# A fused attention block: set-up rebuilt, two GpSimd chains and a new plan

## The chip, the cores and the metric

The kernel runs on one NeuronCore of a Trainium2 chip. The metric is the time of one execution on the device in microseconds. Before the change it is 406.25 us, the median of three runs (406.25 to 406.31). The profile shows one execution, from its first to its last instruction.

## The reference

x is 1 x 2048 x 448 in bf16, with 16 heads of 28 columns each:

```python
qkv = (x @ wqkv).reshape(B, S, 3, H, Dh).transpose(2, 0, 3, 1, 4)
q, k, v = qkv[0], qkv[1], qkv[2]
scores = einsum("bhqd,bhkd->bhqk", q, k) * Dh ** -0.5
p = softmax(scores, axis=-1)
o = einsum("bhqk,bhkd->bhqd", p, v)
return o.transpose(0, 2, 1, 3).reshape(B, S, D) @ wo
```

## The kernel before

**Tiling.** The heads stand in 4 groups of 4, each head padded to 32 rows. The 2048 queries are 4 blocks of 512. A window is one group and one query block, so there are 16 windows; each has 16 key tiles of 128, and for each key tile 4 heads. A score tile is 128 keys by 512 queries of one head: 1024 tiles in all. TensorE (PE) computes a tile with one matmul over 64 rows (L935): 32 rows are the head's key and query, the other 32 hold the absolute query and a negative bound on the key, so that the score arrives with an upper bound already subtracted and no row maximum is needed. After the exponential a matmul with the values (L1203) adds into the bank PO. A column of ones in the values gives the denominators.

**Three ways to the exponential.** Most tiles go in pairs through a PA bank pair, and ScalarE (ACT) takes the exponential of 128x1024 (L1364, into PTA). A part goes through a PD bank: VectorE (DVE) makes two passes of a polynomial (DU L1139, DV L1142), GpSimd (POOL) multiplies (DG L1145), and DVE finishes into PTD (L1158). For the third kind DVE only copies the score into SG (L1071) and GpSimd does the rest as a chain of six: GU (L1078), GE (L1081), GV (L1084), GU (L1086), SG (L1088), PTD (L1101). `start_g` makes that chain. There is one set of GU, GV, GE, so one chain at a time (`GMAX = 1`, `NG = 3` copies of SG), and none starts before 40 tiles have been issued (`GBEG`).

**Set-up.** The blocks of x are called b = 0 to 3. Blocks 0 to 2 are loaded as XS and transposed by PE (L462) into XT; block 3 comes transposed by DMA. The loads are issued on SP's queue (x0, WQ, x1, x2, WV, block 3), WK alone on ACT's queue. GpSimd pads WK into WKP (L425), ACT pads WQ into WQP (L426). DVE fills constants before, among them the unit rows of XT and the ones in VA (L359, L360). For key block 0, PE makes K (L578) and Q (L714), DVE reduces the largest |k| to KPART (L587), ACT copies the two Q halves (L730, L732) and the two masked key copies (L599, L596); DVE and GpSimd form |q| times the bound into QB (L738, L749, L746). The first two windows run first over key block 0 alone, four heads for each key tile; the bound over all keys (KMAX L630, NK L635) follows while they run, and DMAs copy keys and bound rows to the other partitions (L641, L652). `task_factor` (FW, negm, RR L997) corrects the first two partial sums to the common bound.

**Order.** Nothing is scheduled by hand. While the program is built, an event loop plays the whole kernel through: each `Op` has an engine, a length, the latency of its result, and what it depends on; per-window numbers in `PLAN` set priorities, leads and thresholds. At each instant `try_pe`, `try_act` and `try_static` choose an instruction for a free engine, and the order so found is what each engine executes. On the chip, semaphores keep the dependencies, and each engine works through its list in order. At a POOL operation the loop adds `TDEP` where it follows the one it depends on. A DVE operation of kind `sb` (SBUF to SBUF, such as QP) and a GpSimd operation are kept apart by `port` and `lock`.

**End.** The last window normalizes on DVE by transposes (L947 to L1509), and the remaining output matmuls use banks that have come free; ACT and DVE copy, SP and ACT issue the stores.

```python
op = Op("ACT", 0.0633 + 0.4267 * len(ns), fn, kind="E", lat=ELAT)
cp = add(Op("DVE", CPY, lambda: nc.vector.tensor_copy(out=X[:], in_=PX[slot.idx][:]), deps=[sop], ...))
if o.kind == "g" and (pool_last[0] in o.deps or o.dur == PTS and o.acq is None):
    o.dur += TDEP
```

Of the kernel before, what the change touches and what calls it, by code (L numbers as in the profile page):

```python
# [21 lines left out]
P = 128  # L22
# [10 lines left out]
KEPS = 1e-6  # L33
# [19 lines left out]
    "LEADC": [30, 0, 39, 26, 16, 30, 14, 14, 37, -2, 23, 43, 34, 20, -3, 13],  # L53
    "PVMORE": [3, 9, 6, 1, 2, 5, 3, 4, 4, 3, 2, 6, 2, 2, 0, 8],
    "QFROM": [8, 0, 13, -18, 2, -7, -14, -3, -29, 0, 15, -30, 2, 27, 2, 20],
    "QBY": [64, 33, 84, 35, 80, 63, 48, 35, 70, 68, 37, 26, 24, 83, 73, 82],
    "QLEAD": [-88, 27, 38, -61, -3, -56, 48, 32, 6, -83, 0, 17, 28, -85, -90, 11],
    "KFROM": [34, 11, 29, -12, -10, -8, 19, 19, 18, 30, 41, -14, 27, 26, 8, 2],
    "KBY": [23, 12, 48, -4, 29, 50, 40, 54, 30, -2, 2, 49, 14, 48, 9, 40],
    "KLEAD": [34, 27, -74, -63, -7, -50, 32, 24, 1, -25, -43, -62, 18, -27, -8, 47],  # L60
    "VFROM": [-2, 8, 7, 30, -2, 49, 8, 15, 40, -1, -5, 24, 46, -9, 35, 43],
    "VBY": [41, 25, 52, 0, 56, 14, 11, 57, 57, 37, 59, 4, 57, -8, 17, 49],
    "VLEAD": [48, 73, 0, -21, 9, -23, 6, 54, 46, 20, 21, -27, -34, 9, -21, -1],
    "NORM": [20, 10, -10, 38, 6, 40, 20, 10, -14, -4, 9, -10, -18, 20, 32, -1],
    "TAIL": [8, 8, 40, 1],
    "PART": [-34, -19, 34, 37, -30, 40, 3, 30],
    "OUT": [0, 10, 28, 39, 20, -22, 7, -6, 5, -8, -2, 39, -30, -10, 13, 39],
    "SLK": [0.2, 0.22, 0.21, 0.19, 0.12, 0.21, 0.2, 0.12, 0.24, 0.11, 0.08, 0.22, 0.17, 0.19, 0.27, 0.12],
# [6 lines left out]
TDEP = 0.12  # L75
WDR = 0.117
VREL = 0.3
# [10 lines left out]
EVU = 0.598  # L88
DISS = 0.6
# [6 lines left out]
class Op:  # L96
    __slots__ = ("eng", "dur", "lat", "deps", "fn", "prio", "elig", "acq", "rel", "end", "start", "kind", "after")

    def __init__(self, eng, dur, fn, deps=(), prio=0.0, elig=None, acq=None, rel=None, lat=SEM, kind=None, after=None):
        self.eng, self.dur, self.fn, self.deps, self.prio = eng, dur, fn, list(deps), prio  # L100
        self.elig, self.acq, self.rel, self.lat, self.kind, self.after = elig, acq, rel, lat, kind, after
        self.end = None
        self.start = None
# [14 lines left out]
def kernel(  # L118
# [29 lines left out]
    NG = 3  # L148
    GMAX = 1
# [6 lines left out]
    GBEG = 40  # L156
# [35 lines left out]
    FE2 = 80  # L192
# [3 lines left out]
    TE = 0  # L196
    CPE = 1
    REDP = 0
    TW = 0
    XLAT = (4.6, 7.3, 8.9, 9.6)  # L200
    WQLAT = 5.9
    XSP = 1
    KP0 = -4377
    KP1 = -4375
    KP2 = -4485
    BP2 = 34
    PBND = ((3,), (2, 3))
    VE = 16
    UV = 4
    BW = (-1, 4, 1)  # L210
    THF = (0, 1, 0, 0)
    EVP = (-1200, -4365, -700, 0)
    KEVP = (0, 200, 200, 200)
    WQE = 'ACT'
    QORD = 0
    KCH = ((1, 2), (2, 4))
    RCH = ((1, 4), (0, 1))
    XT3 = 14.0
    XBAR = True
    KENG = ('ACT', 'DVE', 'DVE', 'DVE')  # L220
    HENG = ('ACT', 'DVE', 'DVE', 'DVE')
# [24 lines left out]
    RK0 = sb([P, 1], F32, "RK0")  # L246
# [3 lines left out]
    VA = [sb([P, NKT, HG, HP], BF16, f"VA{g}") for g in range(G)]  # L250
# [35 lines left out]
    maskm = sb([P, QW], BF16, "maskm")  # L286
# [3 lines left out]
    bndcol = [sb([P, 1], F32, f"bndcol{pr}") for pr in range(2)]  # L290
    mcol = sb([P, 1], F32, "mcol")
    bdiff = sb([P, 1], F32, "bdiff")
    negm = sb([P, NF, HP], BF16, "negm")
# [5 lines left out]
    nc.scalar.dma_start(out=WK[:, :, 0:GW], in_=wq3[:, :, D:D + GW])  # L299
    for b in range(NQC):  # L300
        if b < NQC - 1:
            nc.sync.dma_start(out=XS[b][:], in_=x_perm[:, b * TPC:(b + 1) * TPC, :])
# [23 lines left out]
    for i in range(HG):  # L326
        nc.gpsimd.affine_select(out=onescol[:], in_=onescol[:], compare_op=ALU.not_equal, fill=1.0,
                                base=-(HP * i + Dh), pattern=[[0, 1]], channel_multiplier=1)
    for g in range(G):
# [4 lines left out]
    UB = 96  # L334
# [13 lines left out]
    nc.gpsimd.tensor_scalar(out=mcol[:], in0=onescol[:], scalar1=MARG, scalar2=-MARG, op0=ALU.mult, op1=ALU.add)  # L348
    nc.gpsimd.tensor_tensor(out=bdiff[:], in0=onescol[:], in1=mcol[:], op=ALU.subtract)
    for pr in range(2):  # L350
# [338 lines left out]
    def task_Q(g, c):  # L689
# [30 lines left out]
        if w == 0:  # L720
            k0mm.extend(ops)
# [826 lines left out]
```

## Time and profile before

| what | value |
|---|---|
| time, median of three | 406.25 us |
| span of the profiled execution | 404.5 us |
| first exponential starts | 11.87 us |
| last exponential ends | 396.9 us |
| exponentials on ACT | 419 (418 of 128x1024, one of 128x512) |
| tiles through DVE and GpSimd / through GpSimd alone | 162 / 25 |
| busy: PE, DVE, ACT, POOL | 353.5, 387.5, 393.5, 345.0 us |
| granted TensorE clock | 0.999 |

The profiled execution's own time is not recorded apart from its span; the three timed runs agree within 0.06 us, so the span is set against their median, and 1.75 us lie around it. In a group's row stand line, engine, operation, the written tile, an arrow and the tiles read, shapes and count; then busy microseconds, the mean of one in ns, the idle time just before, and what ended it. A timeline row has start and length in us, then how many instructions follow each other, and in brackets the idle time before and its releaser. Lengths of neighbours overlap by some tens of ns.

### The profile page before, as it was taken

How to read it: one execution, taken by the hardware profiler on the slowest of the kernel's cores; microseconds unless marked ns; L12 is line 12 of the kernel's file. 1: busy time of each engine (PE TensorE's matmuls, PEld its weight loads, DVE VectorE, ACT ScalarE, POOL GpSimd, SP SyncE). 2: the span in 40 equal slices, each digit the busy share in tenths (PEclk: the TensorE clock that was granted, in tenths of full speed). 3: DMA queues.
4: the chain of work that ended last, by engine and by line, in shares of the span. 5: the costliest groups of instructions: out<-in, count | busy, mean ns of one | idle time of the engine just before them, and what ended most of it. 6: DMA issues, size and time to landing. Idle time of an engine off the chain costs nothing.

```text
span 404.5 us, 7615 instructions
## 1 busy us (share of the span) xinstructions
PE 353.5 (87%) x2596; PEld 115.6 (29%) x2607; DVE 387.5 (96%) x700; ACT 393.5 (97%) x432; POOL 345.0 (85%) x370
## 2 busy tenths in 40 slices
PE   7999979998898888899888987888898898989896
PEld 4342332322232232322322232222223322222232
DVE  6989999999999999999999999999999999999995
ACT  5999999999999999999999999999999999999994
POOL 3429999879899889899999899988899997989990
PEclk9999999999999999999999999999999999999999
DMA  9351120212301020110411000010220002001012
GB/s 212 51 85 42 47 55 26 36 44 40 68 2 47 0 53 7 18 41 2 101 39 33 24 20 10 1 48 1 71 56 16 32 2 56 11 26 51 5 69 91
DMA packets 36446, 16.58 MB, mean 41 GB/s; under 512 B 28784, under 2 KB 33136, under 8 KB 36408
## 3 DMA queue, kind: packets, MB, share of 16 engines
q1 hardware_dynamic: 35800, 15.89, 16.8%
q8 instruction: 20, 0.33, 0.3%
q10 hardware_dynamic: 608, 0.22, 0.2%
q14 instruction: 18, 0.15, 0.1%
HBM read 7.44 MB, written 1.97 MB: 23 GB/s over the span
## 4 chain that ended last, share of the span: by engine, by line
ACT 42%; DVE 23%; PE 15%; POOL 10%; issue 7%; DMA 1%; SPq 0%; DVEq 0%; POOLq 0%
ACT PTA L1364 42%; PE PA L935 6%; DVE PTD L1158 6%; DVE DU L1139 5%; DVE DV L1142 5%; POOL DG L1145 5%; PE PO L1203 4%; PE PD L935 2%; POOL GU L1086 1%; POOL SG L1088 1%; PE PO L714 1%; DMA QB<-QP 1%; DVE SG L1071 1%; POOL OSB L1011 1%; POOL PTD L1101 1%
## 5 line engine op out<-in xcount | busy, mean ns | idle before, releaser
L1364 ACT ACTIVATE PTA<-PA 128x1024 bf16<-128x1024 f32 x419 | 384.5, 1165 | 0.8 <-PE PA L935 0.6
L935 PE MATMUL PA<-QB,KB 64*128 64x512 bf16 x837 | 168.5, 381 | 39.5 <-ACT PTA L1364 36.0
L1145 POOL TENSOR_TENSOR DG<-DV,DU 128x512 f16<-128x512 f16 x162 | 185.1, 1154 | 16.8 <-DVE DV L1142 11.9
L935 PEld LDWEIGHTS <-KB 64*128 64x128 bf16 x1024 | 61.5, 93 | 181.7 <-issue 173.6
L1158 DVE SCALAR_TENSOR_TENSOR PTD<-PD,DG 128x512 uint16<-128x512 f32 x162 | 109.0, 679 | 3.1 <-POOL DG L1145 2.0
L1142 DVE SCALAR_TENSOR_TENSOR DV<-PD,DU 128x512 f16<-128x512 uint16 x162 | 107.9, 680 | 0.8
L1139 DVE TENSOR_SCALAR DU<-PD 128x512 f16<-128x512 uint16 x162 | 106.8, 677 | 1.9 <-PE PD L935 1.7
L1203 PE MATMUL PO<-PTA,VA 128*32 128x512 bf16 x837 | 83.1, 385 | 0.1
L935 PE MATMUL PD<-QB,KB 64*128 64x512 bf16 x187 | 68.6, 377 | 3.5 <-DVE PTD L1158 2.0
L1203 PE MATMUL PO<-PTD,VA 128*32 128x512 bf16 x187 | 53.6, 386 | 0.0
L1203 PEld LDWEIGHTS <-VA 128*32 128x32 bf16 x1024 | 18.8, 94 | 46.5 <-issue 44.9
L1086 POOL TENSOR_TENSOR GU<-GV,GU 128x512 f16<-128x512 f16 x25 | 28.9, 1154 | 2.2 <-DVE QP L762 1.5
L1088 POOL TENSOR_TENSOR SG<-SG,GU 128x512 f32<-128x512 f32 x25 | 28.9, 1155 | 1.9 <-DVE QP L762 0.8
L1084 POOL TENSOR_TENSOR GV<-GE,GU 128x512 f16<-128x512 f32 x25 | 28.9, 1156 | 1.7 <-DVE QP L762 0.8
L1038 POOL TENSOR_TENSOR OT<-OSB,RRB 128x512 bf16<-128x512 f32 x15 | 19.0, 1270 | 1.5 <-DVE PTD L1158 1.5
L1078 POOL TENSOR_SCALAR GU<-SG 128x512 f16<-128x512 uint16 x25 | 15.4, 617 | 5.1 <-DVE SG L1071 3.4
L1071 DVE COPY SG<-PD 128x512 f32<-128x512 f32 x25 | 17.0, 681 | 0.5 <-PE PD L935 0.3
L714 PE MATMUL PO<-XT,WQP 112*128 112x512 bf16 (+1 forms) x52 | 16.9, 385 | 0.3 <-DVE OSB L1023 0.3
L1081 POOL TENSOR_SCALAR GE<-SG 128x512 f32<-128x512 uint16 x25 | 15.4, 617 | 2.0
L578 PE MATMUL PO<-XT,WKP 112*128 112x512 bf16 (+1 forms) x52 | 16.9, 385 | 0.1
L794 PEld LDWEIGHTS <-XT 112*128 112x128 bf16 x256 | 13.6, 98 | 10.7 <-issue 10.4
L1101 POOL TENSOR_SCALAR PTD<-SG 128x512 uint16<-128x512 f32 x25 | 15.5, 618 | 0.9
(120 smaller groups left out, 197.4 us busy)
## 6 DMA issues: line engine op xcount, KB each, us to landing
RRB<-SCR SPq DMA_DIRECT2D x15, 256.0 KB
QB<-QP SPq DMA_DIRECT2D x56, 32.0 KB
KB<-NK SPq DMA_DIRECT2D x12, 128.0 KB
XS<-in_x_dram SPq DMA_DIRECT2D x3, 448.0 KB
QB<-QB SPq DMA_DIRECT2D x28, 32.0 KB
out_dram<-XS SPq DMA_DIRECT2D x2, 448.0 KB
KB<-KB SPq DMA_DIRECT2D x6, 128.0 KB
RRB<-SCRF SPq DMA_DIRECT2D x2, 256.0 KB
```

The lines of the kernel that those rows point to most:

```text
L714: ops = chain_mm(CC, lambda cc: nc.tensor.matmul(out=ap(), lhsT=WQP[g][0:rows_of(g, c, cc), cc, :], rhs=XT[c][cc // 2][0:rows_of(g, c, cc) ...
L935: nc.tensor.matmul(out=ap, lhsT=KB[g % 2][i // 2][a:a + 64, j * P:(j + 1) * P], rhs=QB[w % NQB][i // 2][a:a + 64, :], start=True, stop=Tru ...
L1071: cp = add(Op("DVE", CPY, lambda: nc.vector.tensor_copy(out=X[:], in_=PX[slot.idx][:]), deps=[sop], prio=n - PLAN["LEADC"][now()], lat=0.165))
L1084: g3 = add(Op("POOL", PTT, lambda: nc.gpsimd.tensor_tensor(out=GV[:], in0=GE[:], in1=GU[:], op=ALU.mult), deps=[g2], prio=prio + 2, kind=" ...
L1086: g4 = add(Op("POOL", PTT, lambda: nc.gpsimd.tensor_tensor(out=GU[:], in0=GV[:], in1=GU[:], op=ALU.mult), deps=[g3], prio=prio + 3, kind=" ...
L1088: g5 = add(Op("POOL", PST, lambda: nc.gpsimd.tensor_tensor(out=X[:], in0=X[:], in1=GU[:], op=ALU.add), deps=[g4], prio=prio + 4, kind="g", ...
L1139: p1 = add(Op("DVE", P1, lambda: nc.vector.tensor_scalar(out=DU[b][:], in0=lo, scalar1=SIG / 65536, scalar2=SIG * (SS - 0.5), op0=ALU.mult ...
L1142: p2 = add(Op("DVE", P1, lambda: nc.vector.scalar_tensor_tensor(out=DV[b][:], in0=lo, scalar=65536 * (SS - 0.5 + CE / C3), in1=DU[b][:], o ...
L1145: gq = add(Op("POOL", PTT, lambda: nc.gpsimd.tensor_tensor(out=DG[b][:], in0=DV[b][:], in1=DU[b][:], op=ALU.mult), deps=[p2], prio=n, kind ...
L1158: f = add(Op("DVE", P1, lambda: nc.vector.scalar_tensor_tensor(out=PTD[st["s"].idx][:].bitcast(U16), in0=PX[slot.idx][:], scalar=EBITS + C ...
L1203: nc.tensor.matmul(out=PO[HP * st:HP * (st + 1), :], lhsT=VA[g][:, j, st, :], rhs=r["p"][i][1](), start=first, stop=last, tile_position=(0 ...
L1364: nc.scalar.activation(out=PTA[pslot.idx][:, 0:len(ns) * QW], in_=PA[s.idx][:, 0:len(ns) * QW], func=ACT.Exp, bias=ACT_BIAS, scale=ACT_SCALE)
```

## The change

- **Loads.** WK is issued on SP's queue, after x0 and ahead of WQ.
- **Padding and constants.** GpSimd pads WK in two halves and WQ whole. The unit rows of XT and the ones in VA move from DVE to GpSimd, written as 32-bit words; VA has two buffers in place of four, so values of group g wait for the weighted sums of group g-2.
- **Block 0 of x** is transposed and copied in four column pieces, three copied by DVE and one by ACT, and each key and query matmul waits for its piece alone.
- **Bounds.** The first block's |q| is no longer multiplied by the key bound; the bound is a column (`bndcol`, two sets) which `masked_evac` puts into the key copy, for block 0 by DVE in pieces of 128 and 384 columns, for block 1 by DVE after the overall maximum. Copying key block 1 by DMA falls away; the repeats of NK for it too.
- **Query blocks.** For window 0 ACT evacuates one half and forms |q| of one head; DVE does the others. The second query block is evacuated twice from PSUM instead of copied in SBUF.
- **First windows.** The first two windows run heads 0 and 1 over four key tiles, then heads 2 and 3.
- **GpSimd chains.** Two sets of GU, GV, GE (`NCH = 2`), `GMAX = 2`, `NG = 4`, chains from 58 tiles on.
- **Planner.** A GpSimd operation carries the class of its first scalar (`cls`); a change of class costs `PSW`. Operations of a chain wait for their predecessor's latency. Lists are kept sorted and searched in that order. `PLAN` is new.

```diff
-    nc.scalar.dma_start(out=WK[:, :, 0:GW], in_=wq3[:, :, D:D + GW])
         if b == 0:
+            nc.sync.dma_start(out=WK[:, :, 0:GW], in_=wq3[:, :, D:D + GW])
             nc.sync.dma_start(out=WQ[:, :, 0:GW], in_=wq3[:, :, 0:GW])
...
-    for b in range(NQC - 1):
-        nc.vector.memset(XT[b][1][UB:CK + 2, 1, :], 1.0)
-    nc.vector.memset(VA[0][:].rearrange("p j h e -> p (j h) e")[:, :, Dh:HP], 1.0)
+    nc.gpsimd.memset(XT[0][1][UB:CK + 2, 1, :].bitcast(F32), ONES2)
...
+    for cc in range(CC):
+        tv = xbank[cc].bitcast(BF16)
...
+        tro = add(Op("PE", 0.22, tr0, deps=[xs_in], prio=-5000 + cc, lat=0.1, kind="T"))
...
+        xt_done[0].append(add(Op(XE[cc], 0.41 if XE[cc] == "DVE" else 0.58, ev0, deps=[tro], prio=-5000 + cc, lat=0.08)))
...
+    kpads = [add(Op("POOL", 0.33, pad_half(ch), deps=[wkin], prio=-5001 + 0.1 * ch, lat=0.1)) for ch in range(2)]
+    w_ready[("q", 0)] = add(Op("POOL", 0.57, pad_w(WQ, WQP, 0), deps=[wqin], prio=-4999, lat=0.1))
...
+    def masked_evac(k, sc, ap, dep, kmax, pb, p0, p1):
+        bcs = []
+        for i in range(HG):
+            st = SI[i]
+            eng = nc.gpsimd if k else nc.vector
+            bcs.append(add(Op("POOL" if k else "DVE", 0.21, lambda st=st, eng=eng: eng.tensor_scalar(
+                out=bndcol[k][st % 2][HP * (st ^ 1):HP * ((st ^ 1) + 1), :], in0=kmax[HP * st:HP * (st + 1), :],
+                scalar1=mcol[HP * st:HP * (st + 1), 0:1], scalar2=0.0, op0=ALU.mult, op1=ALU.add), deps=dep, ...
+        def ev(pr, a, b, prio, elig=None):
+            return add(Op("DVE", 0.065 + EVC * (b - a), lambda: nc.vector.tensor_scalar(
+                out=KB[0][pr][:, sc * QW + a:sc * QW + b], in0=ap()[:, a:b], scalar1=selcol[pr][:, 0:1], scalar2=bndcol[k][pr][:, 0:1], op0=ALU.mult, op1=ALU.add),
+                deps=bcs[2 * pr:2 * pr + 2], prio=prio, elig=elig))
+        if k:
+            return [ev(pr, 0, QW, p1 if pr else p0) for pr in range(2)]
+        return [ev(0, 0, P, p0), ev(0, P, QW, -4387.5, ...), ev(1, 0, P, p1), ev(1, P, QW, -4355)]
...
+            ab = add(Op("ACT", 0.62, lambda: nc.scalar.activation(
+                out=QB[0][0][HP:2 * HP, :], in_=ap[0:HP, :], func=ACT.Abs, scale=YSC), deps=[ops[-1]], prio=-4389, lat=0.17))
...
-    KCH = ((1, 2), (2, 4))
-    RCH = ((1, 4), (0, 1))
+    KCH = ((2, 4),)
+    RCH = ((2, 4), (0, 1))
...
-    NG = 3
-    GMAX = 1
+    NG = 4
+    NCH = 2
+    GMAX = 2
...
+        ch = g_seq[0] % NCH
         g_seq[0] += 1
+        U, V, E = GU[ch], GV[ch], GE[ch]
...
-                    if o.kind == "g" and (pool_last[0] in o.deps or o.dur == PTS and o.acq is None):
-                        o.dur += TDEP
+                    if o.cls:
+                        if o.cls != pool_cls[0]:
+                            o.dur += PSW
```

More of the change, by code (lines that the diff above doesn't have):

```diff
@@ L533 @@
     rep0s = []
[L534 to L535 removed]
+    k0ev0 = []
+    neg_op = []
     SI = (0, 2, 1, 3)
```

471 lines of the change are left out of this document (230 added, 241 removed), and 6 rows, old and new, of the table PLAN.

## The prediction

> **What bounds the kernel now.** I read the page first (shares, groups), then ScalarE's (ACT's) timeline, then the busy time by stretch, and last the timeline of the set-up.
>
> ```profile
> span 404.5 us, 7615 instructions
> PE 353.5 (87%) x2596; PEld 115.6 (29%) x2607; DVE 387.5 (96%) x700; ACT 393.5 (97%) x432; POOL 345.0 (85%) x370
> L1364 ACT ACTIVATE PTA<-PA 128x1024 bf16<-128x1024 f32 x419 | 384.5, 1165 | 0.8 <-PE PA L935 0.6
> L1145 POOL TENSOR_TENSOR DG<-DV,DU 128x512 f16<-128x512 f16 x162 | 185.1, 1154 | 16.8 <-DVE DV L1142 11.9
> L1142 DVE SCALAR_TENSOR_TENSOR DV<-PD,DU 128x512 f16<-128x512 uint16 x162 | 107.9, 680 | 0.8
> L1084 POOL TENSOR_TENSOR GV<-GE,GU 128x512 f16<-128x512 f32 x25 | 28.9, 1156 | 1.7 <-DVE QP L762 0.8
> L1078 POOL TENSOR_SCALAR GU<-SG 128x512 f16<-128x512 uint16 x25 | 15.4, 617 | 5.1 <-DVE SG L1071 3.4
> L1071 DVE COPY SG<-PD 128x512 f32<-128x512 f32 x25 | 17.0, 681 | 0.5 <-PE PD L935 0.3
> ```
>
> ```profile
> 11.87 24.26 ACT L1364 ACTIVATE PTA<-PA 128x1024 bf16<-128x1024 f32 x26 [0.62 <-PE PA L935]
> 35.98 0.65 ACT L997 ACTIVATE RR<-PO 128x512 f32<-128x512 f32 x1
> 36.45 360.44 ACT L1364 ACTIVATE PTA<-PA 128x1024 bf16<-128x1024 f32 x393
> 398.22 0.53 ACT L898 CAST XS<-PA 128x448 bf16<-128x448 f32 x1 [1.33 <-PE PA L897]
> ```
>
> ```profile
> 37.00:387.00 350.00, 307.32 (x2244) 97.41 (x2254) 344.66 (x596) 349.88 (x383) 320.42 (x318) 1.00 0.13 32
> ```
>
> The 1024 score tiles have three ways to their exponential: in pairs on ACT (419 instructions), through DVE and GpSimd together (162 tiles), through one DVE copy and then GpSimd alone (25). From 11.87 us to 36.45 + 360.44 = 396.89 us ACT does nothing but exponentials, one per 360.44 / 393 = 0.917 us, with a single other instruction (L997) between. So the span is three terms: 11.87 us until the first exponential, 385.0 us of them, and 7.6 us of tail. The last fence (columns: PE, weight loads, DVE, ACT, POOL busy) shows what stands close behind: in 350 us DVE is idle for 5.3 us, GpSimd for 29.6 us. The granted clock is 1.00.
>
> **The change, term by term.**
>
> *1. Until the first exponential.* These rows carry the set-up:
>
> ```profile
> 0.73 0.42 ACTq L299 DMA_DIRECT2D WK<-in_wqkv_dram  x1
> 0.74 0.40 SPq L302 DMA_DIRECT2D XS<-in_x_dram  x1
> 4.56 1.57 DVE L359 MEMSET XT<- 18x512 bf16 x3
> 4.64 0.88 PE L462 MATMUL PD<-ident,XS 128*112 128x128 bf16 x12 [0.17 <-DMA XS<-in_x_dram]
> 5.09 0.56 POOL L425 COPY WKP<-WK 112x448 bf16<-112x448 bf16 x1 [0.36 <-DVE XT L359]
> 5.98 0.58 ACT L475 COPY XT<-PD 112x512 bf16<-112x512 bf16 x1
> 6.23 0.27 DVE L360 MEMSET VA<- 128x256 bf16 x1
> 6.42 0.63 DVE L473 COPY XT<-PD 112x1024 bf16<-112x1024 bf16 x1
> 6.96 0.41 DVE L473 COPY XT<-PA 112x512 bf16<-112x512 bf16 x1
> 7.10 0.59 PE L578 MATMUL PD<-XT,WKP 112*128 112x512 bf16 x2 [1.36 <-DVE XT L473]
> 7.53 1.02 PE L714 MATMUL PD<-XT,WQP 112*128 112x512 bf16 x4
> 8.39 0.59 PE L578 MATMUL PD<-XT,WKP 112*128 112x512 bf16 x2
> 8.59 0.69 ACT L730 ACTIVATE QB<-PD,offscol 128x512 bf16<-128x512 f32 x1 [2.03 <-PE PD L714]
> 8.82 0.61 PE L462 MATMUL PA<-ident,XS 128*112 128x128 bf16 x8
> 9.02 0.69 DVE L587 TENSOR_REDUCE KPART<-PD 128x1 f32<-128x512 f32 x1 [1.65 <-PE PD L578]
> 9.18 0.68 ACT L732 ACTIVATE QB<-PD,offscol 128x512 bf16<-128x512 f32 x1
> 9.83 0.15 DVE L592 TENSOR_SCALAR KPART<-KPART 128x1 f32<-128x1 f32 x1
> 10.01 1.79 DVE L749 TENSOR_SCALAR QB<-QP,KPART 32x512 bf16<-32x512 bf16 x3
> 10.48 0.77 ACT L596 ACTIVATE KB<-PD,bndcol,selcol 128x512 bf16<-128x512 f32 x1
> 11.46 0.37 PE L935 MATMUL PA<-QB,KB 64*128 64x512 bf16 x1 [0.37 <-DVE QB L749]
> ```
>
> The transposes of x start at 4.64, when it has landed; WK's 98 KB run beside it, from ACT's queue. Behind x they leave it alone: nothing gained at the least, at the most WK's share at the rate of that moment,
>
> ```profile
> 3.00:4.00 1.00, 1.00 (x4) 0.36 (x3) 0.93 (x7) 1.00 (x1) 0.72 (x6) 1.00 1.06 327
> ```
>
> 98 KB / 327 GB/s = 0.3 us. I take 0.2: start at 4.44. The price is WK itself, which now lands after x; its padding (0.56 us, halved into two) could end 0.5 us later than 5.65 and still precede the use below.
>
> Now DVE's four memsets (4.56 to 6.50) stand before its first copy of transposed x. They go to GpSimd (the first block's ahead of time, the rest behind the weight padding), so DVE copies as the transposes come. Sixteen of them take 0.88 + 0.39 less overlap, 1.1 us, four to a column piece: the pieces are there at about 4.9, 5.1, 5.3 and 5.6; DVE copies three (0.41 each), ACT one (0.58), and the last ends at 6.07 against 7.37 now. The key matmuls follow (their order puts all four ahead of the query's) and end at 6.1 + 0.4 = 6.55 against 8.98. The absolute maximum (0.69) ends at 7.3. Two small bound columns (0.15 each as in L592) and a 128-column piece of the key copy, a quarter of a 0.7 us copy plus its fixed part, say 0.25, end near 8.0 on DVE. That was 0.78 + 0.77 on ACT.
>
> On the other branch the four query matmuls (1.02) end at 7.4; ACT evacuates the first half (0.69, to 8.15) and takes |q| for one head, 0.6 behind it as L732 stands 0.59 behind L730: 8.75. This replaces QP, the floor and the multiplications by the key bound, 1.79 for three. The first score pair runs at 8.8, and the exponential follows 11.87 - 11.46 = 0.41 later: **9.3 us, a gain of 2.6**. Earliest 8.9 (copies hidden better, WK's whole 0.3). Latest 9.9: PE's order puts eight transposes of the second x block (0.61 us) ahead of the first score matmul, and their rows show that block landed only by 8.82.
>
> *2. Does it stay fed?* From the maximum at 6.6 to the key copies of block 1, which the 17th exponential needs, DVE's order holds some 32 instructions: twelve copies and evacuations and three maxima of 0.6, two key pieces of 0.5, ten short ones of 0.1 to 0.3; about 13 us. Their scores must run one exponential ahead, at 9.3 + 15 x 0.917 = 23.1. That leaves 3.5 us for waits, so I put zero; at most 1.0, since three waits for PE or GpSimd (the four bound columns it computes after the overall maximum) stand in the row. The eight repeat DMAs become four of 32x8x128 and four late ones; four copies fewer pass SP. They are off the path as long as SP's first key copies leave by 22.
>
> *3. Number of exponentials.* 417 whole ones instead of 418 and one of half width; tiles on DVE with GpSimd 161, on GpSimd alone 29. One whole is 0.917; the half lies between 0 and 0.92, I take 0.5: **-1.4**, with ends -0.9 and -1.8. L997 stays on ACT.
>
> *4. What DVE pays.* Four more copies less three passes, each 0.68: +0.7. In the stretch above it has 5.3 idle, and the stretch shrinks by 1.4: 3.2 stay. If 3.2 suffices, nothing; if it must keep its 5.3, 2.1. ACT has waited 0.8 us in all for 419 instructions, so I stay near the low end: **+0.5**.
>
> *5. What GpSimd pays.* A chain is three of 0.617 and three of 1.155, 5.3 us; four more less one DG are +20.1. Its idle 29.6 becomes 29.6 - 20.1 - 1.4 = 8.1 us in some 349. Two chains on buffers of their own let an unrelated instruction stand between dependent ones; no row here prices that alone, so zero to a few us back. The planner's count of first-scalar changes adds no instruction, only order. I take no loss, since GpSimd is not the last link of the tail now:
>
> ```profile
> 391.00 3.38 POOL L1145 TENSOR_TENSOR DG<-DV,DU 128x512 f16<-128x512 f16 x3
> ```
>
> It is done at 394.4, 2.5 us ahead of ACT. In the new order one P·V tile behind the last exponential waits for GpSimd's very last instruction, so that cover is what is spent first.
>
> *Sum.* Tail unchanged (7.6). Span 404.5 - 2.6 - 1.4 + 0.5 = 401.0. The time is 406.25 for a span of 404.5, so 1.75 lies around it: **402.8 us**.
>
> **The rivals.**
>
> *GpSimd becomes the bound (slower).* Against its remaining 8.1 us of idle stand its waits today:
>
> ```profile
> POOL DG L1145 <- DVE DV L1142: 11.9, 28, 0.8
> POOL DG L1145 <- DVE QP L762: 3.7, 5, 1.5
> POOL GU L1086 <- DVE QP L762: 1.5, 3, 0.8
> ```
>
> They make 17.1 us. If GpSimd goes on waiting so long, it ends 9.0 us late: 402.3 (without the 0.5) + 9.0 = 411.3. It decides from 4 us of lost idle on, where the set-up's gain is used up. Against it: while GpSimd has slack such waits cost nothing and are not avoided, and with two chains there is other work to put there. The Trainium skill, page SBUF — State Buffer, section Who interferes with whom, speaks against the change here: a DVE instruction in a two-port mode takes the port pair that it shares with GpSimd for its whole length, and GpSimd stands still. The trace agrees in kind, as the waits behind QP (SBUF to SBUF, 16-bit) show, though the kernel also orders these two itself; by that rule the 14 remaining QP instructions cost GpSimd what they do now, 5.2 us in these two rows, out of 8.1.
>
> *DVE takes the gain back.* It needs the 5.3 idle and the early feed breaks for 1.0: 402.3 + 2.1 + 1.0 = 405.4. For it: 98% busy. Against: the same passes, less per exponential than before.
>
> *The set-up does half of what it says.* x lands no earlier, and the second x block's transposes hold up the score matmul: first exponential at 10.6, 404.1.
>
> *ACT is fed better.* The chain of waits has a stretch in which nothing holds it:
>
> ```profile
> 12.89 9.28 ACT PTA L1364 x10
> ```
>
> (9.28 - 1.165) / 9 = 0.902. At half the way from 0.917, 416 intervals give 3.1 back: 399.7.
>
> **How the numbers follow.** Forecast 0.54 (401 to 404), GpSimd 0.13, DVE 0.16, half a set-up 0.09, better fed 0.08. A measurement of this kernel tells about 0.2%, 0.8 us, from no change, so faster is below 405.4. Forecast, half set-up and better fed are faster (0.71); DVE's case lies across that bound: 0.08 faster, 0.05 same, 0.03 slower; GpSimd's is slower. Faster 0.79, same 0.05, slower 0.16. From 400.8 to 407.0 lie most of the forecast, DVE's case, the half set-up and the mild part of GpSimd's.
>
> **What will show it.** Right: DVE's copies of x begin below 5 us, the key maximum near 6.6, the first exponential at 9.0 to 9.6, ACT without a gap over 1 us until 36, 417 exponentials at 0.915 to 0.92, GpSimd above 96% from 37 us on and finished before ACT. Wrong: score matmuls that wait for DVE's PTD or GpSimd's GU or SG, an ACT row whose idle time grows from 0.8 to several us, or a last P·V tile waiting for GpSimd with PE idle behind ACT's end.

## The result and the profile after

The changed kernel takes **403.19 us** (median of five runs, 402.86 to 403.44), against 406.25 us (five runs, 406.25 to 406.31): a ratio of 0.9923, with a 95% interval of [0.9911, 0.9935]. That is 3.06 us less, and 0.4 us above the forecast of 402.8. The profiled execution is the fastest of the five: 402.86 us with a span of 401.0; the others have spans of 401.2 to 401.7. Of all the executions named below one lies far off, 937.78 us for the kernel with less work on GpSimd, whose other four take 402.30 to 403.38; it is left out, and its reason isn't known.

The page of the changed kernel, shares and costliest groups:

```profile
span 401.0 us, 7584 instructions
PE 351.0 (88%) x2591; PEld 112.6 (28%) x2602; DVE 387.3 (97%) x704; ACT 390.7 (97%) x427; POOL 360.2 (90%) x399
DVE 43%; ACT 20%; POOL 19%; PE 9%; issue 6%; DMA 2%; SPq 0%; DVEq 0%; POOLq 0%; ACTq 0%
L1380 ACT ACTIVATE PTA<-PA 128x1024 bf16<-128x1024 f32 x417 | 383.4, 1125 | 0.9 <-PE PA L949 0.7
L1158 POOL TENSOR_TENSOR DG<-DV,DU 128x512 f16<-128x512 f16 x161 | 183.9, 1159 | 10.0 <-DVE DV L1155 7.3
L1171 DVE SCALAR_TENSOR_TENSOR PTD<-PD,DG 128x512 uint16<-128x512 f32 x161 | 108.6, 679 | 4.1 <-POOL DG L1158 3.7
L949 PE MATMUL PD<-QB,KB 64*128 64x512 bf16 x190 | 70.5, 376 | 5.6 <-DVE PTD L1171 4.5
```

The same two rows of the kernel before, the chain and the score matmuls into PD banks:

```profile
ACT 42%; DVE 23%; PE 15%; POOL 10%; issue 7%; DMA 1%; SPq 0%; DVEq 0%; POOLq 0%
L935 PE MATMUL PD<-QB,KB 64*128 64x512 bf16 x187 | 68.6, 377 | 3.5 <-DVE PTD L1158 2.0
```

GpSimd has 15 us more work than before and DVE the same; ACT's own idle time is still below 1 us. The lines that begin with an engine and its share are the chain that ended last: ACT's share of it has fallen from 42% to 20%, and DVE and GpSimd now make 62% of it in place of 33%. The three engines stand so close together that the chain jumps from one to the other. Score matmuls into PD banks wait 4.5 us for DVE's last pass in place of 2.0.

ACT's timeline of the changed kernel (start, length, then count of instructions that follow each other):

```profile
9.21 21.24 ACT L1380 ACTIVATE PTA<-PA 128x1024 bf16<-128x1024 f32 x23 [0.49 <-PE PA L949]
30.44 0.60 ACT L1011 ACTIVATE RR<-PD 128x512 f32<-128x512 f32 x1
30.93 332.89 ACT L1380 ACTIVATE PTA<-PA 128x1024 bf16<-128x1024 f32 x362
364.01 29.45 ACT L1380 ACTIVATE PTA<-PA 128x1024 bf16<-128x1024 f32 x32 [0.19 <-PE PA L949]
394.96 0.53 ACT L908 CAST XS<-PA 128x448 bf16<-128x448 f32 x1 [1.50 <-PE PA L907]
```

The last exponential ends at 364.01 + 29.45 = 393.46 us. So the span's three terms are:

| term | before | after | difference |
|---|---|---|---|
| until the first exponential | 11.87 | 9.21 | -2.66 |
| first exponential to end of last | 385.02 | 384.25 | -0.77 |
| tail | 7.6 | 7.6 | 0.0 |

The busy time by stretch of the changed kernel (PE, weight loads, DVE, ACT, POOL):

```profile
37.00:385.00 348.00, 306.03 (x2260) 94.75 (x2270) 343.54 (x594) 347.59 (x380) 337.58 (x341) 1.00 0.13 32
```

In these 348 us DVE is idle for 4.5 us and GpSimd for 10.4 us (it is busy 97.0%). The set-up, from the timeline of the changed kernel:

```profile
4.38 0.88 PE L443 MATMUL PD<-ident,XS 128*112 128x128 bf16 x12
4.84 0.87 DVE L449 COPY XT<-PD 112x512 bf16<-112x512 bf16 x2 [0.92 <-PE PD L443]
5.32 1.19 PE L592 MATMUL PD<-XT,WKP 112*128 112x512 bf16 x4
5.63 0.41 DVE L449 COPY XT<-PA 112x512 bf16<-112x512 bf16 x1
6.55 0.69 DVE L601 TENSOR_REDUCE KPART<-PD 128x1 f32<-128x512 f32 x1 [0.50 <-PE PD L592]
7.21 0.61 PE L463 MATMUL PD<-ident,XS 128*112 128x128 bf16 x8
7.81 0.41 DVE L569 TENSOR_SCALAR KB<-PD,selcol,bndcol 128x128 bf16<-128x128 f32 x1
8.13 0.59 ACT L719 ACTIVATE QB<-PD 32x512 bf16<-32x512 f32 x1
8.77 0.93 PE L949 MATMUL PA<-QB,KB 64*128 64x512 bf16 x4 [0.95 <-ACT QB L719]
```

DVE stands ready when the first transposes end, the four key matmuls follow the copies, and the score matmul waits for the |q| that ACT forms (QB L719, the last row's releaser).

### The profile page after: what moved, and what is told of

Read it like the earlier page. It is cut to its first block, busy times and chain, and to the rows that moved or that the text cites. A ratio compares the mean times of both kernels' runs of the same rounds, so it can differ in the third digit from the quotient of the medians.

```text
span 401.0 us, 7584 instructions
## 1 busy us (share of the span) xinstructions
PE 351.0 (88%) x2591; PEld 112.6 (28%) x2602; DVE 387.3 (97%) x704; ACT 390.7 (97%) x427; POOL 360.2 (90%) x399
## 4 chain that ended last, share of the span: by engine, by line
DVE 43%; ACT 20%; POOL 19%; PE 9%; issue 6%; DMA 2%; SPq 0%; DVEq 0%; POOLq 0%; ACTq 0%
ACT PTA L1380 20%; DVE PTD L1171 12%; DVE DU L1152 11%; DVE DV L1155 11%; POOL DG L1158 9%; PE PA L949 3%; PE PO L1216 3%; POOL SG L1104 2%; POOL GU L1102 2%; DVE SG L1087 2%; POOL OT L1052 2%; POOL GV L1100 2%; POOL PTD L1117 1%; DVE VA L820 1%; DMA XS<-in_x_dram 1%
## 5 line engine op out<-in xcount | busy, mean ns | idle before, releaser
L1380 ACT ACTIVATE PTA<-PA 128x1024 bf16<-128x1024 f32 x417 | 383.4, 1125 | 0.9 <-PE PA L949 0.7
L949 PEld LDWEIGHTS <-KB 64*128 64x128 bf16 x1024 | 58.6, 93 | 177.9 <-issue 167.5
L1216 PE MATMUL PO<-PTA,VA 128*32 128x512 bf16 x834 | 85.2, 386 | 0.5 <-DVE VA L820 0.5
L1216 PE MATMUL PO<-PTD,VA 128*32 128x512 bf16 x190 | 56.1, 386 | 0.4 <-DVE KB L623 0.3
L1216 PEld LDWEIGHTS <-VA 128*32 128x32 bf16 x1024 | 20.0, 94 | 56.5 <-issue 55.1
L1102 POOL TENSOR_TENSOR GU<-GV,GU 128x512 f16<-128x512 f16 x29 | 33.6, 1159 | 0.9 <-DVE QP L776 0.8
L1104 POOL TENSOR_TENSOR SG<-SG,GU 128x512 f32<-128x512 f32 x29 | 33.7, 1161 | 0.4 <-DVE QP L776 0.3
L1100 POOL TENSOR_TENSOR GV<-GE,GU 128x512 f16<-128x512 f32 x29 | 33.6, 1159 | 0.1
L1094 POOL TENSOR_SCALAR GU<-SG 128x512 f16<-128x512 uint16 x29 | 17.9, 621 | 2.2
L1097 POOL TENSOR_SCALAR GE<-SG 128x512 f32<-128x512 uint16 x29 | 17.9, 621 | 2.0 <-DVE QP L776 0.2
L1087 DVE COPY SG<-PD 128x512 f32<-128x512 f32 x29 | 19.7, 678 | 0.0
L1117 POOL TENSOR_SCALAR PTD<-SG 128x512 uint16<-128x512 f32 x29 | 18.1, 625 | 1.1 <-PE PD L949 0.3
L805 PE MATMUL PO<-WV,XT 112*128 112x112 bf16 x224 | 16.2, 214 | 0.2
L805 PEld LDWEIGHTS <-XT 112*128 112x128 bf16 x256 | 13.3, 98 | 9.0 <-issue 8.8
```

What stands on the lines that cost most here:

```text
L805: nc.tensor.matmul(out=ap()[:, jj * GW:(jj + 1) * GW], lhsT=XT[jq][cc // 2][0:CK, cc % 2, jj * P:(jj + 1) * P], rhs=WV[:, cc, g * GW:(g + ...
L949: nc.tensor.matmul(out=ap, lhsT=KB[g % 2][i // 2][a:a + 64, j * P:(j + 1) * P], rhs=QB[w % NQB][i // 2][a:a + 64, :], start=True, stop=Tru ...
L1100: g3 = add(Op("POOL", PTT, lambda: nc.gpsimd.tensor_tensor(out=V[:], in0=E[:], in1=U[:], op=ALU.mult), deps=[g1, g2], prio=prio + 2, kind= ...
L1102: g4 = add(Op("POOL", PTT, lambda: nc.gpsimd.tensor_tensor(out=U[:], in0=V[:], in1=U[:], op=ALU.mult), deps=[g3], prio=prio + 3, kind="h", ...
L1104: g5 = add(Op("POOL", PST, lambda: nc.gpsimd.tensor_tensor(out=X[:], in0=X[:], in1=U[:], op=ALU.add), deps=[g4], prio=prio + 4, kind="h", ...
L1216: nc.tensor.matmul(out=PO[HP * st:HP * (st + 1), :], lhsT=VA[g % 2][:, j, st, :], rhs=r["p"][i][1](), start=first, stop=last, tile_positio ...
```

## The experiments

In what follows *excess* is a number worked out from the trace: the start of the last exponential minus the start of the first, minus 0.902 us for each step between. It collects what ACT loses to late score tiles, and whatever else lengthens a step. It is 7.15 us before (418 steps) and 7.85 after (416 steps). The page's idle time, 0.8 and 0.9 us, shows little of it, because one exponential's length (1125 ns in the mean) reaches some 0.2 us over into the next one's step. If each step over 0.908 us is set down to what the trace names just before it, steps that a wait ended hold 1.5 us of the excess before and 2.2 after; 4.8 and 4.5 us lie in steps that no wait ended, 0.5 and 0.6 in the step with ACT's one other instruction, and the rest in the shorter steps.

### The set-up

**WK on ACT's queue again.**

```diff
+    nc.scalar.dma_start(out=WK[:, :, 0:GW], in_=wq3[:, :, D:D + GW])
     for b in range(NQC):
...
-            nc.sync.dma_start(out=WK[:, :, 0:GW], in_=wq3[:, :, D:D + GW])
```

> The changed kernel, with WK's load back on ACT's queue beside the first x block; the order of all other instructions stays. Theory (WK's share delays x, 0.2 us taken, 0.3 at most): x's transposes begin at about 4.6 instead of 4.38, the first exponential at about 9.4 instead of 9.21, time about 403.4. Rival (x lands when it lands; WK moved for nothing): transposes at 4.38, time 403.2, or a little less because WK is there earlier.

Measured: 403.25 us (402.84 to 403.48), ratio 0.9924 [0.9910, 0.9937]. This is the time of the changed kernel. In the profiled execution (span 401.5) x landed later:

```profile
4.91 0.88 PE L443 MATMUL PD<-ident,XS 128*112 128x128 bf16 x12 [0.69 <-DMA XS<-in_x_dram]
9.74 1.94 ACT L1380 ACTIVATE PTA<-PA 128x1024 bf16<-128x1024 f32 x2 [0.49 <-PE PA L949]
```

That 4.91 alone would speak for the move of WK, but the kernels that keep the changed kernel's loads start these transposes anywhere from 4.38 to 4.87. One profile doesn't separate the two, and the medians don't either.

**Unit rows and ones on DVE again.** The GpSimd memsets of these tiles go, and DVE's come back ahead of the loop.

```diff
-    nc.gpsimd.memset(XT[0][1][UB:CK + 2, 1, :].bitcast(F32), ONES2)
...
+    for b in range(NQC - 1):
+        nc.vector.memset(XT[b][1][UB:CK + 2, 1, :], 1.0)
+    nc.vector.memset(VA[0][:].rearrange("p j h e -> p (j h) e")[:, :, Dh:HP], 1.0)
```

> The changed kernel, with the unit rows of XT and the ones of the first VA buffer written by DVE before the loop, as before the change; all else in the same order. Theory (DVE's four memsets held the first copies of transposed x): DVE's copies begin near 5.9 instead of 4.84 and follow each other, the key maximum starts near 7.5 instead of 6.55, the first exponential near 10.2, time about 404.1 to 404.2. Rival (the query branch through ACT or the loads set the first exponential): below 0.3 us more.

Measured: 403.64 us (403.56 to 403.77), ratio 0.9936 [0.9923, 0.9948]. From this kernel's timeline:

```profile
4.08 1.57 DVE L350 MEMSET XT<- 18x512 bf16 x3
4.87 0.88 PE L445 MATMUL PD<-ident,XS 128*112 128x128 bf16 x12 [0.47 <-DMA XS<-in_x_dram]
5.93 0.69 DVE L451 COPY XT<-PD 112x512 bf16<-112x512 bf16 x2
10.08 1.94 ACT L1382 ACTIVATE PTA<-PA 128x1024 bf16<-128x1024 f32 x2 [0.49 <-PE PA L951]
```

DVE is at its memsets until its copies begin at 5.93, and the first exponential comes at 10.08. The median is 0.45 us higher, and the five runs now lie within 0.21 us where the changed kernel's lie within 0.58. In this trace DVE is the last to be ready, behind the first transposes; without the memsets the transposes set the start. That their scatter is then what shows in the time fits the two spreads.

**The first x block over two queues** (together with the earlier NK repeats, below).

```diff
+            if b == 0:
+                hf = TPC // 2
+                nc.scalar.dma_start(out=XS[b][:, hf:TPC, :], in_=x_perm[:, hf:TPC, :])
+                nc.sync.dma_start(out=XS[b][:, 0:hf, :], in_=x_perm[:, 0:hf, :])
+            else:
...
```

> The changed kernel with two edits: the repeats of the new key block are issued ahead of its key copies (as tried alone before), and the load of the first x block is split in halves over two queues, SP and ACT. Theory (the landing of x is what is left of the set-up, and its jitter of some 0.5 us reaches the end): if two queues land the block sooner or more evenly, the transposes start at 4.4 or before in the profiled run, the first exponential at 9.2 or before, and the median falls to 402.4 to 402.8 us. Rival (all queues share the same DMA engines, so the block lands when its bytes are through): 402.7 to 403.3 us, as in the kernel with the first edit alone (402.95), with the same spread of about 1 us.

Measured: 403.38 us (403.18 to 403.91), ratio 0.9931 [0.9918, 0.9945]. The transposes start at 4.76, the first exponential at 9.77. That is within the range of the kernels that load the block over one queue, and the median doesn't fall; it lies 0.1 us above the rival's range, with a spread of 0.73.

**What scatters the start.** Twelve of the profiled executions here have the changed set-up or one that leaves its compute as it is. In seven of them the twelve transposes take 0.88 us, and there the first exponential follows their start by 4.83 or 4.84 us (changed kernel: 4.38 and 9.21; WK on ACT: 4.91 and 9.74). In the other five they take longer. From the timeline of the kernel with the NK repeats ahead:

```profile
4.44 1.53 PE L443 MATMUL PD<-ident,XS 128*112 128x128 bf16 x12
9.91 2.85 ACT L1380 ACTIVATE PTA<-PA 128x1024 bf16<-128x1024 f32 x3 [0.49 <-PE PA L949]
```

The same half microsecond by its busy time and clock, first in this kernel, then in the changed one (the first two groups are PE and its weight loads, the last three columns the granted clock, the DMA share and GB/s):

```profile
4.50:5.00 0.50, 0.50 (x5) 0.50 (x6) 0.00 (x0) 0.00 (x0) 0.10 (x1) 1.00 0.54 121
```

```profile
4.50:5.00 0.50, 0.50 (x11) 0.50 (x12) 0.16 (x1) 0.00 (x0) 0.20 (x1) 1.00 0.63 159
```

PE transposes half as many pieces, about 0.1 us for one in place of 0.05, with the granted clock at 1.00 in both, so that the column doesn't show the difference. In the trace the starts lie 107 or 56 ns apart, and in three kernels the step changes from the one to the other within the twelve. The worst case is the kernel with the old plan (further down):

```profile
4.50 1.53 PE L443 MATMUL PD<-ident,XS 128*112 128x128 bf16 x12
10.34 26.72 ACT L1380 ACTIVATE PTA<-PA 128x1024 bf16<-128x1024 f32 x29 [0.49 <-PE PA L949]
```

The Trainium skill, page TensorE: Matmul & The Clock Gate, sections What you observe and What's actually happening, gives 107 and 56 ns for matmuls of 128 columns before and after PE has warmed up, and says that the moment of the change varies by half a microsecond from run to run, since the window that decides it runs freely. The traces agree in both numbers; here the change comes between the warm-up matmuls and somewhat past 6 us, where PE is on the path. In the kernel before, DVE's memsets ended at 6.50, and its first copy waited for them, so there was room ahead of it for both scatters; its five runs lie within 0.06 us.

A later start does reach the end. The three kernels with WK on ACT, with x split and with the NK repeats ahead keep the order of the rest; in their profiled executions the first exponential comes 0.53 to 0.70 us later than in the changed kernel's, and the spans are 0.43 to 0.55 us longer.

### DVE and GpSimd against ACT

Four kernels add work behind 40 us or take it away behind 30 us, and a fifth takes it away from both engines. Added is a maximum over a constant tile on DVE, eight times in all, and a product of the same tile on GpSimd, eight times; nothing reads the results. (The last of DVE's eight runs at 395 us, in the tail.)

```diff
+        if o.eng == "DVE" and o.start > 40:
+            steady[0] += 1
+            if steady[0] % 75 == 0 and steady[0] <= 8 * 75:
+                nc.vector.tensor_reduce(out=xtra[:], in_=zrow[:], axis=AX.X, op=ALU.max)
```

> The changed kernel, with eight extra maxima over a constant 128x512 tile on DVE, one after every 75 of its instructions from about 40 us on (nobody waits for them); about 0.58 us each, 4.6 us in all, as much as DVE's idle time of 4.5 us from 37 to 385 us. Theory (DVE stands next behind ACT): at least half of it shows, time 405.5 to 407.8. Rival (its idle time is usable slack and ACT alone binds): at most 0.5 us more, 403.7.

```diff
+        if o.eng == "POOL" and o.start > 40:
+            steady[0] += 1
+            if steady[0] % 40 == 0 and steady[0] <= 8 * 40:
+                nc.gpsimd.tensor_scalar(out=xtra[:], in0=zrow[:], scalar1=1.0, scalar2=0.0, op0=ALU.mult, op1=ALU.add)
```

> The changed kernel, with eight extra scalar operations over a constant 128x512 tile on GpSimd, one after every 40 of its instructions from about 40 us on (nobody waits for them); about 0.6 us each, 4.9 us in all, against 10.4 us of idle time from 37 to 385 us. Theory (GpSimd still has slack): 0 to 0.7 us more, up to 403.9. Rival (GpSimd has become the bound, its idle time cannot be used): 2.5 to 4.9 us more, 405.7 to 408.1.

Taken away are seven eighths of the key maxima of groups 1 to 3 on DVE (the bound then covers 64 of 512 columns), and seven eighths of GE on GpSimd (the rest of GE holds ones, not older values as the expectation says).

```diff
-                out=KPART[g][:, sc:sc + 1], in_=KB[g % 2][0][:, cs], axis=AX.X, op=ALU.max, apply_absolute_value=True),
+                out=KPART[g][:, sc:sc + 1], in_=KB[g % 2][0][:, sc * QW:sc * QW + 64], axis=AX.X, op=ALU.max, apply_absolute_value=True),
```

> The changed kernel, but the twelve key maxima of groups 1 to 3 (on DVE) look at the first 64 columns of each 512 only, so part of the reduction is left out; same order. DVE has about 12 x 0.5 = 6 us less to do. Theory A (after the change GpSimd is the engine that ACT runs against, DVE only second): at most 0.8 us less than 403.2. Theory B (DVE alone holds ACT back): 1.5 to 3 us less, about 401. The first exponential is to stay between 9.2 and 9.8.

```diff
-            out=E[:], in0=lo, scalar1=1.0, scalar2=65536 * (SS - 0.5 + CE / C3), op0=ALU.mult, op1=ALU.add),
+            out=E[:, 0:64], in0=lo[:, 0:64], scalar1=1.0, scalar2=65536 * (SS - 0.5 + CE / C3), op0=ALU.mult, op1=ALU.add),
```

> The changed kernel, but GE of the GpSimd chains is computed for the first 64 columns of 512 only (the rest keeps older values), so those tiles leave work out; same order. GpSimd has about 29 x 0.5 = 14 us less to do. Theory A (GpSimd is the engine that ACT runs against): 0.8 to 2.5 us less than 403.2, and GpSimd ends some us ahead of ACT instead of 0.2. Theory B (DVE alone): 0 to 0.3 us less.

Both of the last two edits in one kernel:

> Work is left out on both helpers of ScalarE at once: DVE takes its key maxima over 64 of 512 columns (some 6 us less work) and GpSimd computes its tile GE over 64 of 512 columns (some 14 us less). Each alone gave 0.1 us or less. Theory (ScalarE itself is the bound; both helpers merely keep pace with it): 402.6 to 403.2 us, with the excess of the exponentials over 0.902 us at 7 or above. Rival (each helper covers for the other, so that only relief of both shows): 401.5 us or less, with the excess below 6.

Measured, with the work as the groups' busy time shows it (GE: 17.9 us after, 7.0 where it is cut; key maxima 8.0 and 2.5):

| kernel | DVE | GpSimd | median, us | to the changed kernel | ratio to before | excess |
|---|---|---|---|---|---|---|
| DVE more | +5.4 | | 406.34 | +3.15 | 1.0001 [0.9992, 1.0010] | 10.65 |
| GpSimd more | | +4.9 | 407.54 | +4.35 | 1.0034 [1.0021, 1.0047] | 12.00 |
| DVE less | -5.5 | | 403.05 | -0.14 | 0.9924 [0.9911, 0.9937] | 7.50 |
| GpSimd less | | -10.9 | 403.14 | -0.05 | 0.9920 [0.9907, 0.9932] | 7.14 |
| both less | -5.5 | -10.9 | 402.40 | -0.79 | 0.9905 [0.9891, 0.9919] | 6.92 |

The groups of the kernel with more on GpSimd:

```profile
L1381 ACT ACTIVATE PTA<-PA 128x1024 bf16<-128x1024 f32 x417 | 385.4, 1090 | 2.8 <-PE PA L950 1.8
L1172 DVE SCALAR_TENSOR_TENSOR PTD<-PD,DG 128x512 uint16<-128x512 f32 x161 | 109.3, 683 | 7.0 <-POOL DG L1159 6.6
L950 PE MATMUL PD<-QB,KB 64*128 64x512 bf16 x190 | 70.5, 376 | 11.3 <-DVE PTD L1172 9.5 <-DVE SG L1088 0.6
L1518 POOL TENSOR_SCALAR xtra<-zrow 128x512 f16<-128x512 bf16 x8 | 4.9, 617 | 0.1
```

The extra instructions take 4.9 us of GpSimd; DVE's last pass then waits 6.6 us for GpSimd in place of 3.7, PE waits 9.5 us for a PD bank to come free in place of 4.5, and ACT's score tiles come late. In the stretch from 37 to 385 us this GpSimd is as busy as the changed kernel's:

```profile
37.00:385.00 348.00, 303.51 (x2241) 91.84 (x2251) 340.83 (x588) 345.76 (x375) 337.62 (x345) 1.00 0.13 32
```

337.62 us against 337.58. So the 10.4 us in which GpSimd doesn't compute are no reserve for work put at these places of its list: they stay, and the whole plan moves back. The kernel that is relieved on both sides:

```profile
37.00:385.00 348.00, 305.07 (x2265) 95.13 (x2273) 341.14 (x596) 347.90 (x380) 329.88 (x343) 1.00 0.13 33
```

GpSimd has 18 us of idle time here and DVE 6.9, and the time falls by 0.79. Neither of the theories about a single bound holds alone. Each microsecond of added work on a helper costs 0.6 to 0.9 us. Less work on one of them moves the median by 0.14 us or less, within the scatter of the runs, because ACT with 417 exponentials at 0.902 us and more is the limit there: in the profiled executions steps that a wait ended hold 2.2 us of the changed kernel's excess, 2.0 with less on DVE, 1.7 with less on GpSimd, 1.3 with less on both, and 6.7 with more on GpSimd. The relief of both lies between its two expectations, nearer to the one in which ACT binds: 0.79 us is about what the two helpers together still hold ACT up. The changed kernel stands at a corner, where more work on either helper costs time and less on one of them gains next to none.

### Chains and plan

**One chain in place of two**, and **the new set-up with one chain and the plan numbers of before**. Of the second the expectation says that the charge for a change of the first scalar is the old one; that edit wasn't made, `PSW` is charged in it.

```diff
-    NG = 4
-    NCH = 2
-    GMAX = 2
+    NG = 3
+    NCH = 1
+    GMAX = 1
```

> The changed kernel with one GpSimd chain instead of two (NCH and GMAX 1, three SG buffers); the planner lays the rest out anew with the same plan numbers, which were not tuned for it. It has 418 exponential instructions against 417 of the changed kernel and 419 of the kernel before. Theory (two chains are worth what the count of instructions says): one instruction of 0.915 us more, so 403.2 + 0.9 = 404.1 us (403.6 to 404.6) if ScalarE stays fed. Rival (two chains also keep DVE and GpSimd from waiting for each other): the gaps of ScalarE grow as well, 405 us or more, and the sum of what its exponentials take above 0.902 us rises by over 1 us from 7.85. Second rival (the second chain is worth nothing): 403.2 us within 0.4.

> The new set-up with what the kernel before had behind it: one chain, the old plan numbers, the old charge for a change of the first scalar, the old start of the GpSimd tiles. 420 exponential instructions. Theory (the set-up's gain reaches the end of the kernel whole): against the kernel before the first exponential comes 2.3 us sooner (9.55 in place of 11.87, the usual one of the changed kernel's profiled runs) and one instruction more costs 0.9, so 406.25 - 2.3 + 0.9 = 404.85 us (404.3 to 405.4). Rival (the earlier start is given back, because DVE and GpSimd carry the same work and now have less slack to do it in): 406 us or more, and the excess of the exponentials over 0.902 us above 9 us.

Measured: 417.97 us (ratio 1.0297 [1.0277, 1.0317]) and 422.57 us (1.0399 [1.0384, 1.0413]). By their numbers both times fall to the rivals (405 and 406 us or more), but not for the rivals' reasons, as the timelines of ACT show. One chain:

```profile
47.74 250.15 ACT L1380 ACTIVATE PTA<-PA 128x1024 bf16<-128x1024 f32 x272 [0.15 <-ACT PTA L1380]
310.55 1.94 ACT L1380 ACTIVATE PTA<-PA 128x1024 bf16<-128x1024 f32 x2 [12.66 <-PE PO L1216]
```

and PE within the hole of 12.66 us, from the timeline of all engines:

```profile
301.52 1.65 PE L805 MATMUL PO<-WV,XT 112*128 112x112 bf16 x16 [0.61 <-DVE QB L758]
303.89 1.28 PE L869 MATMUL PO<-WO,OT 128*128 128x448 bf16 x3 [0.18 <-DVE VA L820]
```

Old plan numbers:

```profile
118.99 1.02 ACT L1380 ACTIVATE PTA<-PA 128x1024 bf16<-128x1024 f32 x1 [8.86 <-PE PA L949]
123.92 2.85 ACT L1380 ACTIVATE PTA<-PA 128x1024 bf16<-128x1024 f32 x3 [3.90 <-PE PA L949]
```

With one chain the excess of the first 312 steps is 5.99 us, against 5.73 in the changed kernel; the next 26 steps add 15.1. ACT has no free PTA there, since PE has value and output matmuls (L805, L869) in its list ahead of the products (L1216) that would free one. With the old numbers the first 104 steps have an excess of 2.10 (changed kernel 2.13), and the next 26 add 13.6; the steps behind them add 7.9, against 5.3 in the changed kernel. So neither kernel prices its part: plan numbers belong to the arrangement for which they were sought, and another one gets an order with a hole in it. What two chains are worth under a plan sought for one stays open; what can be said is that for three quarters of the kernel one chain fed ACT as well.

### Two smaller questions

**The repeats of NK issued ahead of the key copies on SP.** In the changed kernel the weights of the score matmul at 30.30 us wait 0.42 us for them.

```diff
+    log = [(nk0[0].start + 1e-4 if o in rep0s[0:HG] else t, seq, o) for t, seq, o in log]
     log.sort(key=lambda e: (e[0], e[1]))
```

> The changed kernel, with SP issuing the four repeats of NK for key blocks 2 and 3 ahead of the four key copies (NK is ready 0.8 us sooner); else the same order. If the two long gaps of ACT near 28 and 30 us (0.3 and 0.1 us beyond the exponential and the one other instruction) wait for these DMAs, they close and ACT stands 0.3 to 0.4 us earlier at 36 us. If ACT alone sets the end, the time falls by as much, to 402.8 to 402.9; if GpSimd does (theory A), the end stays within 0.2 us.

Measured: 402.95 us (402.66 to 403.72), ratio 0.9922 [0.9911, 0.9934]; the wait is gone from the trace, the excess is 7.66 in place of 7.85. The median can't be told from 403.19. ACT's two long steps stay: in both kernels the exponential behind L1011 starts 21.72 us after the first one, so this wait didn't cause them, and the condition of the expected gain wasn't met.

**One first scalar for all three scalar operations of a chain.** GU and GE are scaled by the cube root of `C3`, and PTD adds behind a maximum with the same constant, which leaves its value as it is.

```diff
-            out=U[:], in0=lo, scalar1=SIG / 65536, scalar2=SIG * (SS - 0.5), op0=ALU.mult, op1=ALU.add),
+            out=U[:], in0=lo, scalar1=ONE / 65536, scalar2=ONE * (SS - 0.5), op0=ALU.mult, op1=ALU.add),
...
-            out=E[:], in0=lo, scalar1=1.0, scalar2=65536 * (SS - 0.5 + CE / C3), op0=ALU.mult, op1=ALU.add),
+            out=E[:], in0=lo, scalar1=ONE / 65536, scalar2=ONE * (SS - 0.5 + CE / C3), op0=ALU.mult, op1=ALU.add),
...
-            ... in0=X[:], scalar1=1.0, scalar2=EBITS + CK0, op0=ALU.mult, op1=ALU.add), ...
+            ... in0=X[:], scalar1=ONE / 65536, scalar2=EBITS + CK0, op0=ALU.max, op1=ALU.add), ...
```

> The changed kernel, with the three scalar operations of a GpSimd chain rewritten so that their first scalar is the same number: GU and GE both scaled by the cube root of the leading coefficient, and PTD by a maximum with that number (no effect on values that count) before its addition. Same instructions, same order. If a change of the first scalar costs GpSimd about 0.115 us (59 of them: 6.9 us), the step from GU to GE falls from 0.70 to 0.58 us, and with theory A the time falls by 0.5 to 1.5 us, to 401.7 to 402.7. With theory B, or if the change of scalar is not what costs, 403.0 to 403.3.

Measured: 449.37 us, ratio 1.1050 [1.1022, 1.1079]. The maximum on GpSimd is what costs:

```profile
L1118 POOL TENSOR_SCALAR PTD<-SG 128x512 uint16<-128x512 f32 x29 | 55.7, 1919 | 2.3 <-PE PD L950 0.3
```

1919 ns in place of 625 (from start to start into DG 1.88 us in place of 0.58), 29 times: 37.6 us more for GpSimd, and 46 us in the time, with the clock down to 0.946. This is the GpSimd bound of the prediction's first rival, brought about. It also bears on the charge `PSW` of 0.115 us. In the changed kernel GE to GU takes 0.70 us from start to start, and GE to DG 0.58:

```profile
73.92 0.62 POOL L1097 TENSOR_SCALAR GE<-SG 128x512 f32<-128x512 uint16 x1
74.62 0.62 POOL L1094 TENSOR_SCALAR GU<-SG 128x512 f16<-128x512 uint16 x1
76.47 0.62 POOL L1097 TENSOR_SCALAR GE<-SG 128x512 f32<-128x512 uint16 x1
77.05 1.16 POOL L1158 TENSOR_TENSOR DG<-DV,DU 128x512 f16<-128x512 f16 x1
```

With the same first scalar in both, the same two steps are:

```profile
78.26 0.62 POOL L1098 TENSOR_SCALAR GE<-SG 128x512 f32<-128x512 uint16 x1
78.96 0.62 POOL L1095 TENSOR_SCALAR GU<-SG 128x512 f16<-128x512 uint16 x1
80.78 0.62 POOL L1098 TENSOR_SCALAR GE<-SG 128x512 f32<-128x512 uint16 x1
81.48 1.15 POOL L1159 TENSOR_TENSOR DG<-DV,DU 128x512 f16<-128x512 f16 x1
```

0.70 and 0.70: the first scalar is equal and the 0.12 us stays, and it even comes to a step that had none. The whole traces say the same: the 8 steps from GE to GU take 0.70 us in the median in both, the 15 from GE to DG 0.58 and 0.70. So the planner charges something that is there, but a changed first scalar isn't the whole of its cause, and what it is stays open.

## Why the prediction was right, step by step

**1. Until the first exponential: right.** Forecast 9.3 us, profiled 9.21; and each link within 0.25 us: last copy of x ends at 6.04 (6.07 forecast), key matmuls at 6.51 (6.55), maximum at 7.24 (7.3), key piece at 8.22 (8.0), |q| at 8.72 (8.75), first score pair 8.77 (8.8). Putting the memsets back brings 10.08, so 0.9 of the 2.66 us, or 0.4 counted from the start of the transposes, has a run behind it; the rest (the copies by pieces, the bound as a column, |q| without it) is read from the timelines alone. The first sub-term, 0.2 us for WK behind x, is not shown. What the step missed is its scatter: in the profiled executions that leave the set-up's compute as it is, the first exponential lies between 9.21 and 10.34, and the kernel before had the one cover for it, DVE's memsets. The latest end that was given, 9.9, was reached and once passed, by another cause than the second x block's transposes, which ran at 7.21 and held nobody up. The median of the runs lies 0.33 us above the profiled one; that is most of the 0.4 us by which the forecast was low. That a later start reaches the end is shown above; where the other runs of this kernel started is not recorded, so that it is the start that differs in them is argued, not shown.

**2. Does it stay fed: right.** The first 23 exponentials take (21.24 - 1.13) / 22 = 0.914 us each, and between exponentials no gap before 36 us reaches 0.5.

**3 and 4. Number of exponentials, and what DVE pays: right in the sum, -0.77 against -0.9.** The two parts can be read off: two steps fewer are 2 x 0.902 = 1.80, and the last exponential is a whole one of 1.17 us where before it was a half of 0.84, so -1.47 (forecast -1.4). The excess grows from 7.15 to 7.85, +0.70 (forecast +0.5, and put on DVE alone). The experiments don't let it be put on DVE alone: in the profiled executions less work on DVE takes 0.35 us of the excess back, less on GpSimd 0.71 and less on both 0.93, and in the medians only relief of both shows, with 0.79.

**5. What GpSimd pays: the outcome right, the reading behind it wrong.** GpSimd is 97% busy, done 0.2 us before ACT (393.26 against 393.46), and its cover at the end went from 2.5 to 0.2 us as said. But the step treated the 8.1 us of idle time that it worked out as a reserve (10.4 measured, since GpSimd's busy time in the stretch grew by 17.2 us and not by 20.1), and the first rival set the bound at 4 us of it lost. There is no such reserve: 4.9 us more work cost 4.35. The change stopped at the edge, not 8 us ahead of it, and that it lost nothing here was luck as far as this step goes. The prediction also held the Trainium skill's rule on the shared port pair against the change (page SBUF — State Buffer, section Who interferes with whom: a DVE instruction in a two-port mode shuts GpSimd out for its whole length). The rows still show waits behind QP:

```profile
POOL DG L1158 <- DVE QP L776: 2.6, 8, 0.5
POOL GU L1102 <- DVE QP L776: 0.8, 2, 0.5
```

They make 3.4 us in place of the 5.2 that the prediction had carried over, out of the 10.4. The kernel keeps QP and GpSimd apart itself, so these rows don't show the port as their cause, and no run takes the waits away. That 10.9 us less of other work on GpSimd moved the median by 0.05 us speaks against them as what sets the time.

**The rest.** The tail is 7.6 as forecast. 402.86 less the span of 401.05 leaves 1.8 us around it, 1.75 forecast. Of the signs named for being wrong one is there in a mild form: score matmuls wait 4.5 us for DVE's PTD, against 2.0, while ACT's row stays at 0.9. The rival in which ACT is fed better fell: the mean step (0.902 and the excess over the steps) went from 0.919 to 0.921. DVE taking back the gain fell too, with 405.4 us against 403.19, and so did the half set-up, with a first exponential at 10.6, though the worst profiled start, 10.34, comes near it.

## What to carry to other kernels

When two or three engines are each above 96% busy, test the idle time that is left before it is counted as slack: put a few dummy instructions on one engine and take a few off; if adding costs most of what it takes while taking away gives nothing, the plan stands at a corner and the next step must relieve the first engine itself. Read an engine's feed by its start-to-start distance, not by the idle column of its row. Work that is removed from ahead of a DMA's first reader also removes the cover over that DMA's scatter, so expect the median to gain less than the best run.

## What was not expected of the hardware

- Once x's landing is on the path, two things scatter the start: the transposes begin between 4.38 and 4.91 us, and PE runs them at 56 or at 107 ns each, with the granted clock at 1.00 in the two stretches shown. The five runs of the changed kernel spread over 0.58 us, those of the kernel before over 0.06.
- A GpSimd instruction with two scalars takes 1919 ns with a maximum as its first operation, and 625 ns with a product, on the same tile of 128x512. The scalar's value isn't the reason: a product with the same first scalar (GU, GE in that kernel) takes 618 ns or less.
- A GpSimd step is 0.12 us longer beside some pairs of scalar operations (0.70 against 0.58), whether or not their first scalars differ.
